# Attention weights kept for later chunks: turned by VectorE, written to DRAM and read back

## The chip, the cores and the metric

The kernel runs on one core of one Trainium2 chip. The metric is the device time of one execution in microseconds (us). Before the change three executions took 2239.99, 2240.82 and 2241.12 us, median 2240.82 us.

## The reference

Two layers in float32, one after the other. First an attention without softmax over four batches of 3008 rows, in which queries and keys are the same array `z` (64 wide); then a gated feed-forward layer over all 12032 rows:

```
scores = (z @ z.T) / 3008              # per batch, 3008 x 3008
attn   = maximum(scores, 0) ** 2
x      = u * (attn @ v)                # u, v: 3008 x 256
gate   = 1 / (1 + exp(-(x @ w_gate)))  # w_gate, w_val: 256 x 1536
out    = (gate * (x @ w_val)) @ w_out  # w_out: 1536 x 256
```

Since queries and keys are one array, `attn` is symmetric: the block of keys in chunk e against queries in chunk c is the transpose of the block of keys c against queries e.

## The kernel before

**Numbers.** TensorE multiplies in fp32r. To keep float32 accuracy every operand x is split into xh, its value in fp32r, and xl = x - xh, and each product is made of three matmuls (h*h, h*l, l*h). For the scores the two halves of `z` are stacked over the 128 partitions, so that two matmuls do it.

**Tiling.** Each batch has six chunks of 512 queries (the last has 448) and twelve pairs of 256 keys. One step is one (batch b, chunk c, pair k); there are 4 x 6 x 12 = 288 steps. All tiles of attention lie transposed: keys on partitions, queries along the free dimension. The gated layer runs one chunk behind: in step (b, c, k) it does feature block f = k of the chunk before, with 12 blocks of 128 features.

**A step on TensorE**, in this order: scores of the next step (`pe_scores`, L236, 4 matmuls, tile `sc`), attention times v of this step (`pe_pv`, L263, 12 matmuls into `acc`), the output product of an earlier feature block (`pe_out`, L330, 6 matmuls into `oacc`), and gate and value products (`pe_gv`, L297, 12 matmuls into `gv`): 34 matmuls, each with 512 columns (448 where the last chunk is concerned). `sc`, `acc`, `oacc` and `gv` have one PSUM buffer each.

**A step on the other engines**, in this order: ScalarE takes the sigmoid of `gv` and VectorE multiplies (`gate`, L312, tile `g`); for the next step ScalarE does relu and square of `sc` into `r`, VectorE casts `r` to `ah` and subtracts to `al` (`post_scores`, L247); ScalarE copies `g` to `hh` and VectorE subtracts to `hl` (`split_h`, L321). Once per chunk come the transposes of `u` (`prep_u`), the product with `u` (`make_x`), its split (`split_x`) and the transposes of the output (`finish`).

**Order.** The program is written out by hand: each engine takes its instructions in the order of the loop over `steps` (L427). All DMAs go through SP's queue, in that same order. During the first two chunks of batch 0 the weights of the gated layer, which arrive as float64 words, are loaded (`load_w`), narrowed to float32 (`narrow_w`: ScalarE one, VectorE five instructions, GpSimd one) and split (`split_w`: VectorE or ScalarE one, GpSimd one); `w_steps` (L371) says at which steps. In steps 14, 17 and 20 two pieces are narrowed.

**Memory.** The pool `const` holds the weights and, last, the tile `zero`, of 16 floats (64 bytes per partition); all other pools (z, v, `ah`, `al`, `hh`, `xh` and so on) lie behind it, and their tiles are multiples of 512 bytes.

Of the kernel before, what the change touches and what calls it, by code (L numbers as in the profile page):

```python
# [8 lines left out]
F32 = mybir.dt.float32  # L9
F32R = mybir.dt.float32r  # L10
# [3 lines left out]
AF = mybir.ActivationFunctionType  # L14
ALU = mybir.AluOpType
# [13 lines left out]
def kernel(  # L29
# [18 lines left out]
    DQ = z.shape[2]  # L50
# [128 lines left out]
    vraw_t, v_t = {}, {}  # L179
# [12 lines left out]
    def prep_v(b, k):  # L192
        t = vraw_t.pop((b, k))
        vh = vp.tile([P, 2, D], F32R, tag="vh", name="vh")
        vl = vp.tile([P, 2, D], F32R, tag="vl", name="vl")
        split(vh, vl, t, nc.gpsimd)
        v_t[b, k] = vh, vl

    def stack_v(b):
        vh, vl = v_t[b, NPAIR - 1]  # L200
        nc.scalar.activation(vh[64:128, 1, :], f32(vl[64:128, 1, :]), AF.Copy)


    uraw_t, u_t = {}, {}
# [25 lines left out]
    def early(b, c):  # L230
        return (b, c) == (0, 0)


    sc_t, a_t, acc_t, x_t = {}, {}, {}, {}

    def pe_scores(b, c, k):  # L236
        n = chunk(c)
        sc = ps.tile([P, 2, CH], F32, tag="gv" if early(b, c) and k % 2 else "sc", name="sc")
        kP = z_t[b, k // 2][0]
        qP, qQ = z_t[b, c]  # L240
        for j in range(2):
            o = (k % 2) * 256 + j * P
            nc.tensor.matmul(sc[:, j, 0:n], kP[:, o : o + P], qP[:, 0:n], start=True, stop=False)  # L243
            nc.tensor.matmul(sc[:, j, 0:n], kP[:, o : o + P], qQ[:, 0:n], start=False, stop=True)  # L244
        sc_t[b, c, k] = sc

    def post_scores(b, c, k):  # L247
        n = chunk(c)
        sc = sc_t.pop((b, c, k))
        r = one.tile([P, 2, CH], F32, tag="ut" if early(b, c) and k % 2 else "r", name="r")  # L250
        if early(b, c) and k % 3 == 2:
            ah = one.tile([P, 2, CH], F32R, tag="xh", name="ah")
            al = one.tile([P, 2, CH], F32R, tag="xl", name="al")
        else:
            ah = two.tile([P, 2, CH], F32R, tag="ah", name="ah")
            al = two.tile([P, 2, CH], F32R, tag="al", name="al")
        nc.scalar.activation(r[:, :, 0:n], sc[:, :, 0:n], AF.Relu, scale=scale)  # L257
        nc.scalar.activation(r[:, :, 0:n], r[:, :, 0:n], AF.Square)  # L258
        nc.vector.tensor_copy(ah[:, :, 0:n], r[:, :, 0:n])  # L259
        nc.vector.tensor_tensor(al[:, :, 0:n], r[:, :, 0:n], f32(ah[:, :, 0:n]), op=ALU.subtract)  # L260
        a_t[b, c, k] = ah, al

    def pe_pv(b, c, k):  # L263
        n = chunk(c)
# [56 lines left out]
    def split_h(b, c, f):  # L321
        n = chunk(c)
        g = g_t.pop((b, c, f))
        pool, tags = (vp, ("vh", "vl")) if (b, c) == (B - 1, NCH - 1) else (two, ("hh", "hl"))
        hh, hl = (pool.tile([P, CH], F32R, tag=tag, name=tag) for tag in tags)
        split(hh[:, 0:n], hl[:, 0:n], g[:, 0:n])
        h_t[b, c, f] = hh, hl

# [60 lines left out]
    with tc.manual_schedule():  # L389


        zero = const.tile([P, 16], F32, name="zero")
        nc.gpsimd.memset(zero, 0.0)
        nc.scalar.activation(zero, zero, AF.Sigmoid)
        idle = one.tile([P, CH], BF16, tag="ut", name="idle")
        nc.vector.memset(idle, 0.0)
        warm = ps.tile([P, 2, CH], F32, tag="acc", name="warm")

        def keep_warm(n):
            for _ in range(n):  # L400
# [24 lines left out]

        m1 = m2 = None
        for g, (b, c, k) in enumerate(steps):  # L427
            C = b * NCH + c
            ahead = g + (1 if C else 2)
            nxt = steps[ahead] if ahead < len(steps) and g != NPAIR - 1 else None  # L430
            if nxt:
                pe_scores(*nxt)
            if m1:
                gate(*m1)
            if k == 0 and C > 0:
                split_x(*chunks[C - 1])
            if nxt:
                post_scores(*nxt)
            if C == 0:
                if k + 2 < NPAIR:  # L440
                    prep_v(0, k + 2)
                if k + 4 < NPAIR:
                    load_v(0, k + 4)
                if k % 2 == 0 and k // 2 + 4 < NCH:
                    load_z(0, k // 2 + 4)
                if k % 2 == 0 and k // 2 + 2 < NCH:
                    prep_z(0, k // 2 + 2)
                if k % 2 == 1 and k // 2 + 3 < NCH:
# [12 lines left out]
            if m2:
                pe_out(*m2)
            m1, m2 = None, m1
            if C > 0:
                m1 = (*chunks[C - 1], k)
                pe_gv(*m1)

            weights(g)
            if c == NCH - 1 and b + 1 < B:
                if k == 0:  # L470
                    load_z(b + 1, 0)
                if k % 2 == 1:
# [76 lines left out]
```

## Time and profile before

| what | value |
|---|---|
| median of three runs | 2240.82 us |
| profiled execution, its own time | 2239.89 us |
| its span, first to last instruction | 2238.1 us |
| TensorE busy | 2204.5 us, 98%, 9762 matmuls |
| VectorE busy | 1169.5 us, 52% |
| ScalarE busy | 1002.3 us, 45% |
| GpSimd busy | 159.2 us, 7% |
| SP's DMA queue | 52.99 MB, 12.2% of the 16 DMA engines' span |
| mean granted TensorE clock | 0.993 |

Of a busy TensorE the distance from the start of one matmul to the start of the next counts, not the duration of one: matmuls overlap, and one that lasts 0.39 us is followed by the next after 0.23 us. A stretch is read by the starts of its first and last rows. PE is TensorE, DVE VectorE, ACT ScalarE, POOL GpSimd, SP the queue that issues all DMAs.

### The profile page before, as it was taken

The numbers are of one execution on the slowest core, as the hardware profiler recorded it, in microseconds if no ns is written. First come the engines' busy times: TensorE is split into PE (matmuls) and PEld (weight loads), VectorE is DVE, ScalarE is ACT, GpSimd is POOL, SyncE is SP. The second block draws the span as 40 slices with busy tenths as digits, with TensorE's granted clock in tenths as the row PEclk, the third lists the DMA queues.
The fourth block names the chain that finished last, engine by engine and source line by source line (L and its number), as shares of the span: only waits on it lengthen the run. The fifth ranks groups of instructions, "written<-read, shape, count | busy, mean of one in ns | idle before, by whom it ended". The sixth has DMA issues, their size and how long they took to land.

```text
span 2238.1 us, 23860 instructions
## 1 busy us (share of the span) xinstructions
PE 2204.5 (98%) x9762; PEld 1839.5 (82%) x9762; DVE 1169.5 (52%) x1451; ACT 1002.3 (45%) x1304; POOL 159.2 (7%) x107
## 2 busy tenths in 40 slices
PE   8889999999999999999999999999999999999998
PEld 5677888888888888888888888888888888888888
DVE  8996445456444444545644444445555444444543
ACT  6454444455444444435544444444554444444432
POOL 3441000013000000002200000000310000000000
PEclk9999999999999999999999999999999999999999
DMA  4221010021110100103101011010410110101101
GB/s 108 81 76 29 1 19 15 15 55 39 20 18 1 19 5 15 29 1 70 39 5 18 1 19 19 1 29 1 84 29 1 18 19 1 19 1 19 18 1 18
DMA packets 271054, 54.51 MB, mean 24 GB/s; under 512 B 250976, under 2 KB 269408, under 8 KB 270944
## 3 DMA queue, kind: packets, MB, share of 16 engines
q1 hardware_dynamic: 270944, 52.99, 12.2%
q8 instruction: 76, 1.25, 0.2%
q14 instruction: 34, 0.28, 0.0%
HBM read 40.63 MB, written 12.32 MB: 24 GB/s over the span
## 4 chain that ended last, share of the span: by engine, by line
PE 91%; DVE 7%; issue 1%; ACT 1%; DMA 0%; SPq 0%; DVEq 0%
PE gv L306 11%; PE gv L305 11%; PE gv L307 11%; PE acc L277 10%; PE acc L278 10%; PE acc L280 10%; PE oacc L347 6%; PE oacc L346 6%; PE oacc L348 5%; PE sc L243 5%; PE sc L244 5%; DVE al L260 1%; DVE ah L259 1%; DVE hl L82 1%; DVE wa L122 1%
## 5 line engine op out<-in xcount | busy, mean ns | idle before, releaser
L316 ACT ACTIVATE g<-gv 128x512 f32<-128x512 f32 (+1 forms) x288 | 169.4, 588 | 1003.1 <-PE gv L307 977.1
L317 DVE TENSOR_TENSOR g<-gv,g 128x512 f32<-128x512 f32 (+1 forms) x288 | 195.9, 680 | 586.9 <-ACT g L316 586.9
L305 PE MATMUL gv<-xh,wgv_h 128*128 128x512 f32 (+1 forms) x1152 | 449.0, 390 | 9.5 <-DVE g L317 9.4
L278 PE MATMUL acc<-al,vh 128*128 128x512 f32 (+1 forms) x1152 | 446.8, 388 | 6.2 <-DVE al L260 6.2
L306 PE MATMUL gv<-xl,wgv_h 128*128 128x512 f32 (+1 forms) x1152 | 449.3, 390 | 1.5 <-DVE xl L82 1.1
L277 PE MATMUL acc<-ah,vh 128*128 128x512 f32 (+1 forms) x1152 | 446.5, 388 | 3.3 <-DVE ah L259 2.0
L307 PE MATMUL gv<-xh,wgv_l 128*128 128x512 f32 (+1 forms) x1152 | 445.1, 386 | 0.0
L280 PE MATMUL acc<-ah,vl 128*128 128x512 f32 (+1 forms) x1104 | 428.3, 388 | 1.7 <-POOL vl L82 1.7
L259 DVE CAST ah<-r 128x1024 fp32r<-128x1024 f32 (+1 forms) x288 | 205.2, 712 | 420.8 <-ACT r L258 420.8
L260 DVE TENSOR_TENSOR al<-r,ah 128x1024 fp32r<-128x1024 f32 (+1 forms) x288 | 360.3, 1251 | 9.8
L257 ACT ACTIVATE r<-sc 128x1024 f32<-128x1024 f32 (+1 forms) x288 | 290.7, 1009 | 79.7 <-PE sc L244 78.5
L258 ACT ACTIVATE r<-r 128x1024 f32<-128x1024 f32 (+1 forms) x288 | 300.0, 1042 | 9.1
L305 PEld LDWEIGHTS gv<-xh,wgv_h 128*128 128x128 f32 x1152 | 217.6, 189 | 54.9 <-DVE g L317 10.6
L278 PEld LDWEIGHTS acc<-al,vh 128*128 128x128 f32 x1152 | 217.8, 189 | 48.7 <-DVE al L260 7.5
L277 PEld LDWEIGHTS acc<-ah,vh 128*128 128x128 f32 x1152 | 217.9, 189 | 46.0 <-ACT vh L81 2.5
L307 PEld LDWEIGHTS gv<-xh,wgv_l 128*128 128x128 f32 x1152 | 217.4, 189 | 43.7
L306 PEld LDWEIGHTS gv<-xl,wgv_h 128*128 128x128 f32 x1152 | 217.8, 189 | 42.4 <-DVE xl L82 3.4
L280 PEld LDWEIGHTS acc<-ah,vl 128*128 128x128 f32 x1104 | 208.8, 189 | 42.3 <-POOL vl L82 3.1
L243 PE MATMUL sc<-zP 128*128 128x512 f32 (+1 forms) x576 | 223.2, 387 | 4.5 <-DVE zP L174 4.4
L244 PE MATMUL sc<-zQ,zP 128*128 128x512 f32 (+1 forms) x576 | 222.6, 387 | 0.2 <-DVE zQ L175 0.2
L82 DVE TENSOR_TENSOR hl<-g,hh 128x512 fp32r<-128x512 f32 (+1 forms) x276 | 215.3, 780 | 0.7 <-ACT hh L81 0.7
L347 PE MATMUL oacc<-hl,wo_h 128*128 128x512 f32 (+1 forms) x552 | 215.1, 390 | 0.0
(54 smaller groups left out, 1670.3 us busy)
## 6 DMA issues: line engine op xcount, KB each, us to landing
vraw<-in_v_dram SPq DMA_DIRECT2D x44, 256.0 KB, 2.9
uraw<-in_u_dram SPq DMA_DIRECT2D x160, 64.0 KB, 2.4
out_dram<-osb SPq DMA_DIRECT2D x160, 64.0 KB, 2.0
zraw<-in_z_dram SPq DMA_DIRECT2D x80, 64.0 KB, 2.8
wraw<-in_moe_w_gate_dram SPq DMA_DIRECT2D x12, 256.0 KB, 2.7
wraw<-in_moe_w_val_dram SPq DMA_DIRECT2D x12, 256.0 KB, 3.1
wraw<-in_moe_w_out_dram SPq DMA_DIRECT2D x6, 512.0 KB, 3.6
uraw<-in_u_dram SPq DMA_DIRECT2D x32, 56.0 KB, 2.4
```

The lines of the kernel that those rows point to most:

```text
L243: nc.tensor.matmul(sc[:, j, 0:n], kP[:, o : o + P], qP[:, 0:n], start=True, stop=False)
L244: nc.tensor.matmul(sc[:, j, 0:n], kP[:, o : o + P], qQ[:, 0:n], start=False, stop=True)
L257: nc.scalar.activation(r[:, :, 0:n], sc[:, :, 0:n], AF.Relu, scale=scale)
L258: nc.scalar.activation(r[:, :, 0:n], r[:, :, 0:n], AF.Square)
L260: nc.vector.tensor_tensor(al[:, :, 0:n], r[:, :, 0:n], f32(ah[:, :, 0:n]), op=ALU.subtract)
L277: nc.tensor.matmul(o, vh[:, j, ds], ah[:, j, 0:n], start=(k == 0 and j == 0), stop=False)
L278: nc.tensor.matmul(o, vh[:, j, ds], al[:, j, 0:n], start=False, stop=last)
L280: nc.tensor.matmul(o, vl[:, j, ds], ah[:, j, 0:n], start=False, stop=False)
L305: nc.tensor.matmul(o, wh, xh[:, d, 0:n], start=(d == 0), stop=False)
L306: nc.tensor.matmul(o, wh, xl[:, d, 0:n], start=False, stop=False)
L307: nc.tensor.matmul(o, wl, xh[:, d, 0:n], start=False, stop=(d == NB - 1))
L347: nc.tensor.matmul(o, wh, hl[:, 0:n], start=False, stop=False)
```

## The change

The weights `r` of keys in a later chunk e than the queries' chunk c are kept for the time when e is the queries' chunk and c the keys' (`kept`, L80 of the new program; batch 0's chunk 0 keeps nothing). VectorE turns each 32x32 block of the tile (`turn`, two transposes of 128x512 per step), and DMAs of 32x16x32 put the blocks at their transposed places in a DRAM tile, in runs of 128 bytes, eight DMAs per step (six for the last pair, which has 192 keys). When chunk e comes, `load_back` reads each pair's tile in one DMA two steps ahead, and `pe_scores`, relu and square are left out for it (`back`, L84).

That concerns 110 of the 288 steps on either side: 30 of a batch's 72, and 20 in batch 0. The cast to `ah` moves from VectorE to ScalarE in steps that read back and in the whole of batch 0's chunk 1. `r` now has two buffers in all steps. The turned tiles use the buffers of `vraw`. The low part of v's last pair, whose second half is stacked into `vh`, is written in place by GpSimd, with no copy by ScalarE; the pool `vl` has a buffer less. `zero` grows from 64 to 512 bytes per partition, so that the pools behind it start at the same offset modulo 512 as the weights.

```diff
+    def kept(b, c, e):
+        return e > c and (b, c) != (0, 0)
+    def back(b, c, k):
+        return kept(b, k // 2, c)
...
     def pe_scores(b, c, k):
+        if back(b, c, k):
+            return
...
-        r = one.tile([P, 2, CH], F32, tag="ut" if early(b, c) and k % 2 else "r", name="r")
+        if back(b, c, k):
+            r = r_t.pop((b, c, k))
+        else:
+            r = two.tile([P, 2, CH], F32, tag="r", name="r")
+            nc.scalar.activation(r[:, :, 0:n], sc[:, :, 0:n], AF.Relu, scale=scale)
+            nc.scalar.activation(r[:, :, 0:n], r[:, :, 0:n], AF.Square)
...
-        nc.scalar.activation(r[:, :, 0:n], sc[:, :, 0:n], AF.Relu, scale=scale)
-        nc.scalar.activation(r[:, :, 0:n], r[:, :, 0:n], AF.Square)
-        nc.vector.tensor_copy(ah[:, :, 0:n], r[:, :, 0:n])
+        if back(b, c, k) or (b, c) == (0, 1):
+            nc.scalar.activation(ah[:, :, 0:n], r[:, :, 0:n], AF.Copy)
+        else:
+            nc.vector.tensor_copy(ah[:, :, 0:n], r[:, :, 0:n])
...
+    def turn(b, c, k):
+        r = r_t.pop((b, c, k))
+        e = k // 2
+        if not kept(b, c, e):
+            return
+        if (b, c, e) not in turned_t:
+            turned_t[b, c, e] = dram.tile([CH, CH], F32, name=f"turned_{b}_{c}_{e}")
+        rows = turned_t[b, c, e].rearrange("(T p) q -> p T q", p=32)
+        for j in range(2):
+            t = two.tile([P, CH], F32, tag="vraw", name="turned")
+            nc.vector.transpose(out=t, in_=r[:, j, :])
+            for g in range(4):
+                q = (k % 2) * 256 + j * P + 32 * g
+                if q < chunk(e):
+                    nc.sync.dma_start(
+                        rows[:, :, q : q + 32],
+                        t[32 * g : 32 * g + 32].rearrange("p (T q) -> p T q", q=32),
+                    )
+    def load_back(b, c, k):
+        n = chunk(c)
+        r = two.tile([P, 2, CH], F32, tag="r", name="r")
+        src = turned_t[b, k // 2, c][(k % 2) * 256 : (k % 2) * 256 + 256, 0:n]
+        nc.sync.dma_start(r[:, :, 0:n], src.rearrange("(j p) q -> p j q", p=P))
+        r_t[b, c, k] = r
...
-        zero = const.tile([P, 16], F32, name="zero")
+        zero = const.tile([P, 128], F32, name="zero")
...
             if nxt:
                 post_scores(*nxt)
+            if g + 2 < len(steps) and back(*steps[g + 2]):
+                load_back(*steps[g + 2])
...
             if m1:
                 split_h(*m1)
+            if nxt:
+                turn(*nxt)
             pe_pv(b, c, k)
```

TensorE, where batch 0's chunk 2 begins to read back; first before (L307 `pe_gv`, L243 and L244 `pe_scores`, L277 to L280 `pe_pv`):

```order
L307 MATMUL gv<-xh,wgv_l 128x512
L243 MATMUL sc<-zP 128x512
L244 MATMUL sc<-zQ,zP 128x512
L243 MATMUL sc<-zP 128x512
L244 MATMUL sc<-zQ,zP 128x512
L277 MATMUL acc<-ah,vh 128x512
```

Now, at the same place (L361 `pe_gv`, L331 to L334 `pe_pv`):

```order
L361 MATMUL gv<-xh,wgv_l 128x512
L331 MATMUL acc<-ah,vh 128x512
L332 MATMUL acc<-al,vh 128x512
L334 MATMUL acc<-ah,vl 128x512
L331 MATMUL acc<-ah,vh 128x512
```

The four matmuls of the scores are gone from between the two products; the rest keeps its order. Over the program TensorE has 440 matmuls fewer.

VectorE, one step of batch 0's chunk 1 in which one weight piece is narrowed, before (L317 `gate`, L259 and L260 `post_scores`, L82 `split_h`, L116 to L126 `narrow_w`):

```order
L317 TENSOR_TENSOR g<-gv,g 128x512
L259 CAST ah<-r 128x1024
L260 TENSOR_TENSOR al<-r,ah 128x1024
L82 TENSOR_TENSOR hl<-g,hh 128x512
L116 TENSOR_SCALAR wa<-wa 128x512
L119 TENSOR_SCALAR wa<-wa 128x512
L122 SCALAR_TENSOR_TENSOR wa<-wraw,wa 128x512
L125 TENSOR_SCALAR wb<-wa 128x512
L126 SCALAR_TENSOR_TENSOR wb<-wraw,wb 128x512
```

The same step now (L371 `gate`, L284 `post_scores`, L95 `split_h`, L301 `turn`, L129 to L139 `narrow_w`):

```order
L371 TENSOR_TENSOR g<-gv,g 128x512
L284 TENSOR_TENSOR al<-r,ah 128x1024
L95 TENSOR_TENSOR hl<-g,hh 128x512
L301 STREAM_TRANSPOSE turned<-r 128x512 x2
L129 TENSOR_SCALAR wa<-wa 128x512
L132 TENSOR_SCALAR wa<-wa 128x512
L135 SCALAR_TENSOR_TENSOR wa<-wraw,wa 128x512
L138 TENSOR_SCALAR wb<-wa 128x512
L139 SCALAR_TENSOR_TENSOR wb<-wraw,wb 128x512
```

The cast has gone to ScalarE, and two transposes stand between `hl` and the weights.

SP's queue at the end of batch 0's chunk 1, before (L92 and L99 `load_w`, L212 `load_u`, L359 `finish`):

```order
L92 DMA wraw<-in_moe_w_gate_dram 128x2x256
L92 DMA wraw<-in_moe_w_val_dram 128x2x256
L212 DMA uraw<-in_u_dram 32x16x32 x8
L99 DMA wraw<-in_moe_w_out_dram 128x2x512
L359 DMA out_dram<-osb 32x16x32 x8
```

The same stretch now (L105 and L112 `load_w`, L305 `turn`, L228 `load_u`, L314 `load_back`, L415 `finish`):

```order
L105 DMA wraw<-in_moe_w_gate_dram 128x2x256
L105 DMA wraw<-in_moe_w_val_dram 128x2x256
L305 DMA turned_1_5_1326<-turned 32x16x32 x8
L228 DMA uraw<-in_u_dram 32x16x32 x8
L112 DMA wraw<-in_moe_w_out_dram 128x2x512
L305 DMA turned_1_5_1326<-turned 32x16x32 x6
L314 DMA r<-turned_1_2_841 128x2x512 x2
L415 DMA out_dram<-osb 32x16x32 x8
```

Eight stores of a turned tile now stand ahead of the loads of u and of the last piece of `w_out`, and two read-backs ahead of the output's stores.

## Rows read from the trace of the kernel before

**Rows 1.** The page's chain that ended last, share of the span by engine.

```profile
PE 91%; DVE 7%; issue 1%; ACT 1%; DMA 0%; SPq 0%; DVEq 0%
```

**Rows 2.** TensorE's waits, first 300 us: us in total, times, longest; the largest.

```profile
PE gv L305 <- DVE g L317: 9.4, 3, 3.3
```

**Rows 3.** TensorE's waits, 300 us to the end: the largest.

```profile
PE gv L306 <- DVE xl L82: 0.7, 1, 0.7
```

**Rows 4.** Timeline, TensorE, one step of 512 columns: start us, us, instruction.

```profile
300.50 0.39 PE L243 MATMUL sc<-zP 128*128 128x512 f32 x1
...
301.41 0.39 PE L277 MATMUL acc<-ah,vh 128*128 128x512 f32 x1
...
304.13 0.39 PE L346 MATMUL oacc<-hh,wo_h 128*128 128x512 f32 x1
...
305.50 0.39 PE L305 MATMUL gv<-xh,wgv_h 128*128 128x512 f32 x1
...
308.25 0.39 PE L243 MATMUL sc<-zP 128*128 128x512 f32 x1
```

**Rows 5.** Timeline, TensorE, a step whose queries are the last chunk.

```profile
1014.68 0.36 PE L243 MATMUL sc<-zP 128*128 128x448 f32 x1
...
1015.49 0.37 PE L277 MATMUL acc<-ah,vh 128*128 128x448 f32 x1
...
1017.97 0.39 PE L346 MATMUL oacc<-hh,wo_h 128*128 128x512 f32 x1
```

**Rows 6.** Timeline, TensorE, gate and value products of a last chunk, and what follows.

```profile
577.93 0.36 PE L305 MATMUL gv<-xh,wgv_h 128*128 128x448 f32 x1
...
580.34 0.39 PE L243 MATMUL sc<-zP 128*128 128x512 f32 x1
```

**Rows 7.** Timeline, VectorE, one steady step; in brackets the idle time before, its releaser.

```profile
305.63 0.68 DVE L82 TENSOR_TENSOR hl<-g,hh 128x512 fp32r<-128x512 f32 x1
309.08 0.69 DVE L317 TENSOR_TENSOR g<-gv,g 128x512 f32<-128x512 f32 x1 [2.76 <-ACT g L316]
```

**Rows 8.** Groups by shape: busy us, mean ns of one, idle before.

```profile
L223 DVE STREAM_TRANSPOSE ut<-uraw 128x512 f32<-128x512 f32 x40 | 25.9, 687 | 0.0
...
L81 ACT ACTIVATE xh<-ut 128x1024 fp32r<-128x1024 f32 x20 | 21.1, 1053 | 8.2 <-DVE ut L285 8.2
```

**Rows 9.** Timeline, SP's queue, the eight stores of one chunk's output.

```profile
198.97 4.16 SPq L359 DMA_DIRECT2D out_dram<-osb  x8
```

**Rows 10.** The page's DMA issues: count, KB each, median us from issue to landing.

```profile
out_dram<-osb SPq DMA_DIRECT2D x160, 64.0 KB, 2.0
...
wraw<-in_moe_w_out_dram SPq DMA_DIRECT2D x6, 512.0 KB, 3.6
```

**Rows 11.** Windows: length, busy of PE, PEld, DVE, ACT, POOL; clock; DMA share, GB/s.

```profile
196.00:204.00 8.00, 8.00 (x37) 6.60 (x36) 4.69 (x7) 3.46 (x5) 0.00 (x0) 1.00 0.40 63
212.00:220.00 8.00, 8.00 (x37) 6.59 (x36) 3.47 (x5) 3.21 (x4) 0.00 (x0) 1.00 0.00 0
```

**Rows 12.** Timeline, VectorE, one step of batch 0's chunk 1 with weights.

```profile
114.86 1.48 DVE L259 CAST ah<-r 128x1024 fp32r<-128x1024 f32 x1
116.37 1.23 DVE L260 TENSOR_TENSOR al<-r,ah 128x1024 fp32r<-128x1024 f32 x1
117.51 1.80 DVE L82 TENSOR_TENSOR hl<-g,hh 128x512 fp32r<-128x512 f32 x1
...
122.02 0.68 DVE L317 TENSOR_TENSOR g<-gv,g 128x512 f32<-128x512 f32 x1
```

**Rows 13.** Timeline, GpSimd, the same step.

```profile
114.49 1.30 POOL L129 TENSOR_TENSOR wa<-wa,wb 128x512 f32<-128x512 f32 x1 [3.40 <-DVE wb L126]
116.53 2.24 POOL L141 TENSOR_TENSOR wo_l<-wa,wo_h 128x512 fp32r<-128x512 f32 x1 [0.74 <-ACT wo_h L140]
```

**Rows 14.** Timeline, SP's queue, the last loads of batch 0's chunk 1.

```profile
161.88 4.05 SPq L212 DMA_DIRECT2D uraw<-in_u_dram  x8
...
170.56 0.38 SPq L99 DMA_DIRECT2D wraw<-in_moe_w_out_dram  x1
```

More of the change, by code (lines that the diff above doesn't have):

```diff
@@ L68 @@
     vp = ctx.enter_context(tc.tile_pool(name="vp", bufs=NPAIR))
+    vlp = ctx.enter_context(tc.tile_pool(name="vlp", bufs=NPAIR - 1))
     ps = ctx.enter_context(tc.tile_pool(name="ps", bufs=1, space=PSUM))
+    dram = ctx.enter_context(tc.tile_pool(name="dram", bufs=1, space=bass.MemoryType.DRAM))
     def f32(ap):
         return ap.bitcast(F32)
+    def kept(b, c, e):
+        return e > c and (b, c) != (0, 0)
+    def back(b, c, k):
+        return kept(b, k // 2, c)
     wgv_h = const.tile([P, NF, 2, NB, P], F32R, name="wgv_h")
@@ L194, in prep_v @@
         vh = vp.tile([P, 2, D], F32R, tag="vh", name="vh")
-        vl = vp.tile([P, 2, D], F32R, tag="vl", name="vl")
-        split(vh, vl, t, nc.gpsimd)
+        if k < NPAIR - 1:
+            vl = vlp.tile([P, 2, D], F32R, tag="vl", name="vl")
+            split(vh, vl, t, nc.gpsimd)
+        else:
+            vl = one.tile([P, 1, D], F32R, tag="vlast", name="vlast")
+            nc.scalar.activation(vh, t, AF.Copy)
+            nc.gpsimd.tensor_tensor(vl[:, 0, :], t[:, 0, :], f32(vh[:, 0, :]), op=ALU.subtract)
+            stacked = vh[64:128, 1, :]
+            nc.gpsimd.tensor_tensor(stacked, t[64:128, 1, :], f32(stacked), op=ALU.subtract)
         v_t[b, k] = vh, vl
-    def stack_v(b):
-        vh, vl = v_t[b, NPAIR - 1]
-        nc.scalar.activation(vh[64:128, 1, :], f32(vl[64:128, 1, :]), AF.Copy)
     uraw_t, u_t = {}, {}
@@ L231, in early @@
         return (b, c) == (0, 0)
-    sc_t, a_t, acc_t, x_t = {}, {}, {}, {}
+    sc_t, r_t, a_t, acc_t, x_t = {}, {}, {}, {}, {}
     def pe_scores(b, c, k):
+        if back(b, c, k):
+            return
         n = chunk(c)
@@ L248, in post_scores @@
         n = chunk(c)
-        sc = sc_t.pop((b, c, k))
-        r = one.tile([P, 2, CH], F32, tag="ut" if early(b, c) and k % 2 else "r", name="r")
+        sc = sc_t.pop((b, c, k), None)
+        if back(b, c, k):
[4 more added lines that the diff above has]
+            nc.scalar.activation(r[:, :, 0:n], r[:, :, 0:n], AF.Square)
         if early(b, c) and k % 3 == 2:
@@ L256, in post_scores @@
             al = two.tile([P, 2, CH], F32R, tag="al", name="al")
-        nc.scalar.activation(r[:, :, 0:n], sc[:, :, 0:n], AF.Relu, scale=scale)
-        nc.scalar.activation(r[:, :, 0:n], r[:, :, 0:n], AF.Square)
-        nc.vector.tensor_copy(ah[:, :, 0:n], r[:, :, 0:n])
+        if back(b, c, k) or (b, c) == (0, 1):
+            nc.scalar.activation(ah[:, :, 0:n], r[:, :, 0:n], AF.Copy)
+        else:
+            nc.vector.tensor_copy(ah[:, :, 0:n], r[:, :, 0:n])
         nc.vector.tensor_tensor(al[:, :, 0:n], r[:, :, 0:n], f32(ah[:, :, 0:n]), op=ALU.subtract)
         a_t[b, c, k] = ah, al
+        r_t[b, c, k] = r
+    turned_t = {}
+    def turn(b, c, k):
[21 more added lines that the diff above has]
+        nc.sync.dma_start(r[:, :, 0:n], src.rearrange("(j p) q -> p j q", p=P))
+        r_t[b, c, k] = r
     def pe_pv(b, c, k):
@@ L323, in split_h @@
         g = g_t.pop((b, c, f))
-        pool, tags = (vp, ("vh", "vl")) if (b, c) == (B - 1, NCH - 1) else (two, ("hh", "hl"))
-        hh, hl = (pool.tile([P, CH], F32R, tag=tag, name=tag) for tag in tags)
+        last = (b, c) == (B - 1, NCH - 1)
+        hh = (vp if last else two).tile([P, CH], F32R, tag="vh" if last else "hh", name="hh")
+        low = last and f < NF - 1
+        hl = (vlp if low else two).tile([P, CH], F32R, tag="vl" if low else "hl", name="hl")
         split(hh[:, 0:n], hl[:, 0:n], g[:, 0:n])
@@ L449 @@
                     turn_z(0, k // 2 + 3)
-                if k == NPAIR - 2:
-                    stack_v(0)
             if m1:
                 split_h(*m1)
+            if nxt:
+                turn(*nxt)
             pe_pv(b, c, k)
@@ L481 @@
                 prep_v(b, NPAIR - 1)
-            if c == 0 and b > 0 and k == 1:
-                stack_v(b)
         last = chunks[-1]
```

## The prediction, made before the changed kernel ran

> **What bounds the kernel now.** I read the chain that ended last first: 91% of the span is TensorE's [rows 1]. TensorE's waits, taken in two stretches, say where it ever stands still: after 300 us its largest wait in total is 0.7 us, while in the first 300 us one kind alone, gate and value products that wait for VectorE's `g`, costs 9.4 us [rows 2, 3]. So there are two regimes. From about 190 us on, the time is the number of matmuls times their distance: one step of 512 columns goes from 300.50 to 308.25, 7.75 us for 34 matmuls, 0.228 us each [rows 4]. VectorE there has 2.76 us of idle time in one piece per step [rows 7]. Before that, in batch 0's chunk 1, VectorE narrows weights and has no gap: from cast to the next `g` its rows follow one another [rows 12].
>
> The window with the eight stores of an output and the one without any DMA both hold 37 matmuls in 8.00 us [rows 11]: transfers cost TensorE nothing there.
>
> **The change part by part.** The sum is made against the profiled execution, 2239.9 us (span 2238.1 and 1.8 around it), 0.9 below the median shown.
>
> *Scores removed.* 110 steps lose 4 matmuls each. Where queries have 512 columns, the four take 301.41 - 300.50 = 0.91 us [rows 4]; in the last chunk 1015.49 - 1014.68 = 0.81 us [rows 5]. Chunk c reads back 2c steps, in batch 0 two fewer from chunk 1 on: 38 steps are of the last chunk (8 + 3 x 10), 72 of the others (12 + 3 x 20). 72 x 0.91 + 38 x 0.81 = 96.3 us. The steady stretch has no other wait to hide behind, so all of it comes off: -96.3.
>
> *What has to stay hidden in steady steps.* VectorE gets two transposes in 110 steps, 2 x 0.687 = 1.37 us [rows 8], directly before its idle 2.76 us [rows 7]. Left are 1.39 us; where the step also transposes u or the output (two more), 2.75 of 2.76 are taken, and `g` behind them still has some 3 us, since its product's next matmul comes at 305.50 + 7.75, and `g` ends at 309.77. Without that cover the price would be 1.37 us x 110 = 151 us. ScalarE loses relu and square in read-back steps and gains one copy of 1.05 us [rows 8]. SP gets eight issues, 4.16 us as for the eight stores of an output, which have the same shape [rows 9], in a step of 7.75; with eight loads of u or eight stores of the output behind them it has some 8.3, and it catches up in the next step, which has 3.6 to spare. The stores land in 2.0 us [rows 10]; the turned tile's two buffers are wanted again one step later, so that from the first transpose 7.75 us are there for 0.69 + 2.1 + 2.0. The read-back has the form of the 512 KB load of `w_out`, 3.6 us [rows 10]. It is issued two steps ahead, behind the wait for the buffer of `r` that `al` or the transposes release; what stands behind it in SP's queue (turned stores, u, output) is not due sooner than half a step later. Its source was stored eight steps before at the nearest. In the read-back step `ah` needs no TensorE, so `al` is early by the 2 us of relu and square. Cost taken: 0; bounds 0 to 5.
>
> On small stores the trace has this: eight of 64 KB in runs of 128 bytes fill 0.40 of the 16 DMA engines over 8 us, 3.2 us of all of them [rows 11], so eight more per step fit in 7.75 us twice. [...]
>
> *Batch 0's chunk 1.* The cast leaves VectorE, but is worth less than its 1.48 us: it starts at 114.86, while GpSimd's addition runs until 115.79 [rows 12, 13], and the next subtraction would wait for GpSimd as well (`hl` takes 1.80 us beside GpSimd's split, 0.68 in a steady step [rows 7, 12]). So 1.48 - 0.93 = 0.55, taken as 0.6, is saved per step, in 11 steps with weights: -6.6. Eight of them gain transposes, 8 x 1.37 = +11.0. In the last such step but one the loads of u and of `w_out` stand behind eight stores: before, u's were issued at 161.88, a step ahead, and `w_out`'s at 170.56 [rows 14]; now SP needs 4.2 for the stores and 4.05 for u, so that the piece lands 0.69 + 4.2 + 4.05 + 3.6 = 12.5 us after the first transpose begins. VectorE wants it a step later: 7.16 from cast to next `g` and 0.6 for `g` [rows 12], 0.8 longer by the change, and behind the next step's transposes and those of u, 2.75: 11.3. That is +1.2, taken as +1.0. Net +5.4. Bounds: -5.3 (11 whole casts of 1.48 gone against 11.0 of transposes) to +12.0 (transposes and late load, nothing saved).
>
> *The 512-byte offset.* `zero` grows, so weights of the gated layer and what is multiplied with them, 64 bytes apart modulo 512 before, agree. In 512-column steps the products whose operands agree already run 12 matmuls in 304.13 - 301.41 = 2.72 us; gate and value take 308.25 - 305.50 = 2.75, the output product's six 1.37 against 1.36 [rows 4]. Brought to the same distance: 0.04 x 240 steps = -9.6. With 448 columns the agreeing ones are the slower: 2.48 for 12 against 2.41 [rows 5, 6], so up to 0.07 and half of it for the output, 0.105 x 48 steps = +5.0. I take both, -4.6; the bounds are the ends, -9.6 and +5.0.
>
> [...]
>
> *The rest.* The copies that stacked v's last pair (one per batch on ScalarE) and the shorter subtraction on GpSimd stand in steps with idle time: 0.
>
> Sum: 2239.9 - 96.3 + 5.4 - 4.6 = **2144.4 us**.
>
> **Rivals.** (A) The offset does nothing. For it: distances differ by about 1% only, and with the opposite sign at 448 columns, so they may belong to the products and not to their addresses. Against: both agreeing products are the quicker at 512 [rows 4]. Time 2149.0. (B) The weights' stretch gets worse: ScalarE's `ah`, behind relu and square, comes when VectorE is free and nothing is saved there, +12.0 in place of +5.4, and the offset gives nothing: 2239.9 - 96.3 + 12.0 = 2155.6. For it: VectorE has no gap there [rows 12]. Against: the cast shows no wait for ScalarE before it [rows 12], so `r` is there early. (C) The other side: the path transpose, eight stores, buffer free becomes the bound of the 110 turned steps. Stores into 2 KB rows of a scratch tile appear nowhere in the trace; the output's go into 1 KB rows. The gain is used up when each turned step is 96.3 / 110 = 0.88 us longer, thus when eight stores take 8.63 us, 2.7 times the 3.2 of [rows 11]. At three times, 9.6 us: 110 x 1.85 = +203, 2347 us. Against: the same run length lands in 2.0 us [rows 10]. (D) The scores are not really saved, because something else sets the step: excluded by 2.76 us of idle on VectorE and by ScalarE's lighter step.
>
> **Numbers.** Forecast 0.55, A 0.32, B 0.09, C 0.04. The low end takes the offset's best and some relief of VectorE: 2239.9 - 96.3 - 9.6 - 3 = 2131. The high end is B with some 2 us for the hidden terms' bound, 2158. This leaves C and the tails out. A measurement of this kernel can tell 0.2% (4.5 us) from no change; all but C are faster by far: faster 0.95, within 0.2% 0.01, slower 0.04.
>
> **What would show it.** TensorE with 440 matmuls fewer and no wait beyond 1 us in total after 200 us per cause; a read-back step of 30 matmuls at 6.84 us. VectorE's idle before `g` in a turned step near 1.4 us. `g`'s wait on TensorE in the first 200 us grown by some 5 us. Twelve gate and value matmuls in 2.72 us, or, for A, still 2.75. The prediction is wrong if turned steps last over 7.75 us, if read-backs release ScalarE's `ah` late, or if SP's queue shows waits for transposes that TensorE's chain ends in.

## The result, and the profile after

The changed kernel takes 2143.05 us (median of four executions, 2141.06 to 2144.6), the kernel before beside it 2240.4 us (2239.92 to 2241.12). The ratio is 0.9565, 95% interval 0.9548 to 0.9581. The profiled execution took 2141.06 us with a span of 2139.2 us; it is the quickest of the four, so that differences read from its stretches and differences of medians can disagree by some 2 us. The forecast was 2144.4 us.

First the page of the changed kernel: busy time and instructions of each engine, the chain that ended last, and the DMA issues that are new.

```profile
PE 2103.4 (98%) x9322; PEld 1755.0 (82%) x9322; DVE 1210.9 (57%) x1549; ACT 895.9 (42%) x1202; POOL 154.9 (7%) x111
...
PE 91%; DVE 4%; ACT 2%; DMA 1%; issue 1%; SPq 1%; POOL 0%; DVEq 0%; ACTq 0%
...
turned<-turned SPq DMA_DIRECT2D x842, 64.0 KB, 1.9
r<-turned SPq DMA_DIRECT2D x72, 512.0 KB, 4.1
```

TensorE has 440 matmuls fewer (9762 before) and still carries 91% of the chain [rows 1]. SP's queue moves three times the bytes, 163.41 MB for 52.99, and stands at 35.8% of the DMA engines for 12.2%. A read-back lands 4.1 us after its issue, where 3.6 were foretold.

To see where the time went, both executions are cut where batch 0's chunks 0 and 1 end (at the start of the split of `x`, `xl`, for the next chunk). Each row below is one stretch: its limits, its length, busy us of PE, PEld, DVE, ACT and POOL with their instructions, granted clock, DMA share, GB/s. Before:

```profile
0.00:79.89 79.89, 64.22 (x226) 45.94 (x227) 70.77 (x79) 42.17 (x53) 33.71 (x25) 0.89 0.43 104
79.89:186.59 106.70, 95.57 (x390) 76.71 (x389) 101.78 (x121) 55.95 (x77) 46.99 (x28) 0.94 0.22 66
186.59:2238.10 2051.51, 2044.73 (x9149) 1716.89 (x9147) 996.97 (x1252) 904.19 (x1176) 78.46 (x54) 1.00 0.11 19
```

After:

```profile
0.00:77.43 77.43, 64.03 (x228) 45.15 (x228) 69.01 (x78) 42.92 (x53) 35.10 (x26) 0.91 0.45 108
77.43:189.03 111.60, 96.04 (x387) 75.97 (x388) 98.62 (x126) 66.83 (x88) 40.80 (x28) 0.94 0.45 104
189.03:2139.20 1950.17, 1943.33 (x8709) 1633.89 (x8707) 1043.31 (x1346) 786.17 (x1063) 78.98 (x57) 1.00 0.35 74
```

Chunk 0 is 2.5 us shorter, chunk 1 4.9 longer, the rest 101.3 shorter, together -98.9. In the rest TensorE is idle for 6.8 us in either kernel (2051.51 - 2044.73, 1950.17 - 1943.33): so its gain is matmuls gone or closer together, although the DMA engines went from 0.11 to 0.35 of their time and VectorE has 46 us more work.

TensorE's waits after, first 300 us, then from 300 us on (total, times, longest):

```profile
PE gv L359 <- DVE g L371: 14.7, 6, 4.6
```

```profile
PE gv L360 <- DVE xl L95: 1.3, 4, 0.7
```

These answer to [rows 2, 3]: 9.4 became 14.7. In the steady stretch 0.7 became 1.3, a little over the 1 us per cause that the forecast had set as a sign, and still nothing worth a term; waits for `g` come to 0.5 us there.

One step of 512 columns on TensorE, to be laid beside [rows 4]:

```profile
320.00 0.39 PE L261 MATMUL sc<-zP 128*128 128x512 f32 x1
...
323.63 0.39 PE L402 MATMUL oacc<-hh,wo_h 128*128 128x512 f32 x1
...
324.99 0.39 PE L359 MATMUL gv<-xh,wgv_h 128*128 128x512 f32 x1
...
327.71 0.39 PE L261 MATMUL sc<-zP 128*128 128x512 f32 x1
```

The step takes 7.71 us for 7.75; gate and value 2.72 for 2.75, the output product 1.36 for 1.37, the rest as before.

VectorE in the steady stretch, to be laid beside [rows 7]: two read-back steps, an ordinary step, a turned step, and one that turns and also transposes `u`. In brackets the idle time before an instruction.

```profile
306.32 0.69 DVE L371 TENSOR_TENSOR g<-gv,g 128x512 f32<-128x512 f32 x1 [4.02 <-ACT g L370]
...
313.12 0.69 DVE L371 TENSOR_TENSOR g<-gv,g 128x512 f32<-128x512 f32 x1 [4.02 <-ACT g L370]
...
328.54 0.69 DVE L371 TENSOR_TENSOR g<-gv,g 128x512 f32<-128x512 f32 x1 [2.72 <-ACT g L370]
...
336.24 0.69 DVE L371 TENSOR_TENSOR g<-gv,g 128x512 f32<-128x512 f32 x1 [1.51 <-ACT g L370]
...
341.14 1.30 DVE L301 STREAM_TRANSPOSE turned<-r 128x512 f32<-128x512 f32 x2
...
343.95 0.69 DVE L371 TENSOR_TENSOR g<-gv,g 128x512 f32<-128x512 f32 x1 [0.32 <-ACT g L370]
```

A read-back step lasts 313.12 - 306.32 = 6.80 us (30 matmuls; 6.84 foretold). The idle piece before `g`, 2.72 in an ordinary step, shrinks to 1.51 in a turned one and to 0.32 where `u` is transposed as well. A piece is left in each of these steps, and TensorE's waits for `g` of 0.5 us in the whole steady stretch say that it is used up hardly anywhere.

Batch 0's chunk 1 is where time was lost. VectorE, one step with weights, beside [rows 12]:

```profile
110.14 0.68 DVE L371 TENSOR_TENSOR g<-gv,g 128x512 f32<-128x512 f32 x1
110.74 1.99 DVE L284 TENSOR_TENSOR al<-r,ah 128x1024 fp32r<-128x1024 f32 x1
...
114.35 1.29 DVE L301 STREAM_TRANSPOSE turned<-r 128x512 f32<-128x512 f32 x2
...
118.58 0.68 DVE L371 TENSOR_TENSOR g<-gv,g 128x512 f32<-128x512 f32 x1
```

From `g` to `g` it is 8.44 us, with no gap over 0.15. The cast of 1.48 is gone, but the subtraction `al` grew from 1.23 to 1.99: it now starts 0.37 after GpSimd's addition, which runs from 110.37 to 111.65. In five other steps of chunk 1 `al` waits for ScalarE's `ah` instead, 5.3 us in all and 1.9 at most; before, VectorE made `ah` itself.

```profile
110.37 1.28 POOL L142 TENSOR_TENSOR wa<-wa,wb 128x512 f32<-128x512 f32 x1 [2.88 <-DVE wb L139]
```

SP's queue at the end of chunk 1, beside [rows 14]: the loads of `u` and `w_out` stand behind eight stores.

```profile
165.75 4.17 SPq L305 DMA_DIRECT2D turned<-turned  x8
170.02 4.17 SPq L228 DMA_DIRECT2D uraw<-in_u_dram  x8
174.30 0.42 SPq L112 DMA_DIRECT2D wraw<-in_moe_w_out_dram  x1
```

The piece of `w_out` is issued at 174.30; VectorE then waits 2.06 us, until 179.04, for ScalarE's first instruction on it. Such waits for weights come to 3.5 us in chunk 1, and one for `u` to 0.4.

### The profile page after: what moved, and what is told of

Its sections match the earlier page's. It is cut to its first block, busy times and chain, and to the rows that moved or that the text cites. A ratio compares the mean times of both kernels' runs of the same rounds, so it can differ in the third digit from the quotient of the medians.

```text
span 2139.2 us, 24723 instructions
## 1 busy us (share of the span) xinstructions
PE 2103.4 (98%) x9322; PEld 1755.0 (82%) x9322; DVE 1210.9 (57%) x1549; ACT 895.9 (42%) x1202; POOL 154.9 (7%) x111
## 3 DMA queue, kind: packets, MB, share of 16 engines
q1 hardware_dynamic: 745440, 163.41, 35.8%
## 4 chain that ended last, share of the span: by engine, by line
PE 91%; DVE 4%; ACT 2%; DMA 1%; issue 1%; SPq 1%; POOL 0%; DVEq 0%; ACTq 0%
PE gv L360 12%; PE gv L359 12%; PE gv L361 12%; PE acc L331 11%; PE acc L332 11%; PE acc L334 10%; PE oacc L403 6%; PE oacc L402 6%; PE oacc L404 6%; PE sc L262 3%; PE sc L261 3%; DVE al L284 1%; DMA wraw<-in_moe_w_val_dram 1%; ACT r L273 0%; ACT r L272 0%
## 5 line engine op out<-in xcount | busy, mean ns | idle before, releaser
L371 DVE TENSOR_TENSOR g<-gv,g 128x512 f32<-128x512 f32 (+1 forms) x288 | 195.7, 679 | 567.1 <-ACT g L370 566.9
L359 PE MATMUL gv<-xh,wgv_h 128*128 128x512 f32 (+1 forms) x1152 | 447.5, 388 | 16.2 <-DVE g L371 15.2
L331 PE MATMUL acc<-ah,vh 128*128 128x512 f32 (+1 forms) x1152 | 446.3, 387 | 1.7 <-DVE ah L283 1.7
L361 PE MATMUL gv<-xh,wgv_l 128*128 128x512 f32 (+1 forms) x1152 | 446.1, 387 | 0.0
L334 PE MATMUL acc<-ah,vl 128*128 128x512 f32 (+1 forms) x1056 | 409.1, 387 | 1.6 <-POOL vl L95 1.6
L284 DVE TENSOR_TENSOR al<-r,ah 128x1024 fp32r<-128x1024 f32 (+1 forms) x288 | 363.7, 1263 | 35.1 <-ACT ah L281 25.3
L359 PEld LDWEIGHTS gv<-xh,wgv_h 128*128 128x128 f32 x1152 | 217.4, 189 | 61.8 <-DVE g L371 19.6
L283 DVE CAST ah<-r 128x1024 fp32r<-128x1024 f32 (+1 forms) x166 | 115.7, 697 | 254.2 <-ACT r L273 254.2
L331 PEld LDWEIGHTS acc<-ah,vh 128*128 128x128 f32 x1152 | 217.5, 189 | 44.7 <-ACT vh L213 1.6
L361 PEld LDWEIGHTS gv<-xh,wgv_l 128*128 128x128 f32 x1152 | 217.5, 189 | 41.1
L334 PEld LDWEIGHTS acc<-ah,vl 128*128 128x128 f32 x1056 | 199.6, 189 | 40.1 <-POOL vl L95 2.7
L403 PE MATMUL oacc<-hl,wo_h 128*128 128x512 f32 (+1 forms) x576 | 222.2, 386 | 0.0
L402 PE MATMUL oacc<-hh,wo_h 128*128 128x512 f32 (+1 forms) x576 | 222.0, 385 | 0.0
L404 PE MATMUL oacc<-hh,wo_l 128*128 128x512 f32 (+1 forms) x576 | 221.9, 385 | 0.0
L95 DVE TENSOR_TENSOR hl<-g,hh 128x512 fp32r<-128x512 f32 (+1 forms) x288 | 215.2, 747 | 9.2 <-ACT hh L94 9.2
L272 ACT ACTIVATE r<-sc 128x1024 f32<-128x1024 f32 (+1 forms) x178 | 181.8, 1021 | 55.7 <-PE sc L262 53.9
L273 ACT ACTIVATE r<-r 128x1024 f32<-128x1024 f32 (+1 forms) x178 | 187.6, 1054 | 5.7
```

Of the source, the lines that this page charges most:

```text
L331: nc.tensor.matmul(o, vh[:, j, ds], ah[:, j, 0:n], start=(k == 0 and j == 0), stop=False)
L334: nc.tensor.matmul(o, vl[:, j, ds], ah[:, j, 0:n], start=False, stop=False)
L359: nc.tensor.matmul(o, wh, xh[:, d, 0:n], start=(d == 0), stop=False)
L361: nc.tensor.matmul(o, wl, xh[:, d, 0:n], start=False, stop=(d == NB - 1))
L371: nc.vector.tensor_tensor(g[:, 0:n], gv[:, 1, 0:n], g[:, 0:n], op=ALU.mult)
L402: nc.tensor.matmul(o, wh, hh[:, 0:n], start=(f == 0), stop=False)
```

## Experiments

My theory was the forecast's sum: scores off TensorE, turning paid for in chunk 1 alone, a small gain from the offset. Each run had the kernel before beside it on the same chip (median 2239.87 us in both groups: e1 to e4, e5 to e8). Differences "to the changed kernel" are to its median of 2143.05 us, lengths of stretches are of the profiled executions, cut as above. Where nothing in the steady stretch was changed, its length repeats within 1.6 us: 1950.17 in the changed kernel, 1948.95 in e3 and 1950.52 in e7.

### e1_offset_back: the changed kernel with `zero` small again

```diff
-        zero = const.tile([P, 128], F32, name="zero")
+        zero = const.tile([P, 16], F32, name="zero")
```

> The changed kernel with the tile zero at 64 bytes again, so that the gated layer's weights and their moving operands differ by 64 bytes modulo 512. Theory (the offset counts): twelve gate and value matmuls of 512 columns go back from 2.72 to 2.75 us and the six of the output from 1.36 to 1.37, those of 448 columns become quicker; 4.6 us more than 2143.1 us, 2147.7. Rival A (the distances belong to the products, not to the offset): 2143.1 us, distances as in the changed kernel.

Measured: 2147.4 us (2146.7 to 2149.74), ratio to before 0.9588 [0.9575, 0.9601], 4.35 more than the changed kernel. TensorE's gate and value products, with 512 and with 448 columns, up to what follows them:

```profile
305.91 0.39 PE L359 MATMUL gv<-xh,wgv_h 128*128 128x512 f32 x1
...
308.66 0.39 PE L331 MATMUL acc<-ah,vh 128*128 128x512 f32 x1
...
580.26 0.36 PE L359 MATMUL gv<-xh,wgv_h 128*128 128x448 f32 x1
...
582.66 0.39 PE L261 MATMUL sc<-zP 128*128 128x512 f32 x1
```

The twelve are back at 2.75 us with 512 columns, and at 2.40 with 448, where the changed kernel has 2.43:

```profile
576.49 0.37 PE L359 MATMUL gv<-xh,wgv_h 128*128 128x448 f32 x1
...
578.92 0.39 PE L261 MATMUL sc<-zP 128*128 128x512 f32 x1
```

The window of the rest, cut at the same place:

```profile
191.54:2147.90 1956.36, 1948.76 (x8709) 1634.19 (x8707) 1042.18 (x1346) 785.82 (x1063) 79.31 (x57) 1.00 0.38 74
```

It has the same 8709 matmuls as the changed kernel and takes 6.2 us longer. Rival A (the offset does nothing) fell.

### e2_offset_alone: the kernel before with the large `zero`

```diff
-        zero = const.tile([P, 16], F32, name="zero")
+        zero = const.tile([P, 128], F32, name="zero")
```

> The kernel before with zero at 512 bytes and nothing else. Theory: 4.6 us less than 2240.4 us, 2235.8, with twelve gate and value matmuls of 512 columns in 2.72 us. Rival A: 2240.4 us, still 2.75.

Measured: 2233.85 us (2233.17 to 2234.59), ratio 0.9972 [0.996, 0.9983], -6.0 us. Its twelve gate and value products of 512 columns take 2.72 us, from the first to what follows, and the window of the rest is cut as before:

```profile
306.05 0.39 PE L305 MATMUL gv<-xh,wgv_h 128*128 128x512 f32 x1
...
308.77 0.39 PE L243 MATMUL sc<-zP 128*128 128x512 f32 x1
```

```profile
187.77:2232.80 2045.03, 2038.00 (x9149) 1717.01 (x9147) 996.68 (x1252) 903.46 (x1176) 78.28 (x54) 1.00 0.10 19
```

The rest is 6.5 us shorter than before with the same 9149 matmuls. Both ways round the offset is worth some 6 us in the steady stretch. The runs know only two cases, 64 bytes apart and in agreement; whether 512 is the measure, or 128 or 256 would do as well, they do not show. e1 and e2 also give the scores by themselves: 2051.51 - 1956.36 = 95.2 us at the old offset, 2045.03 - 1950.17 = 94.9 at the new one.

### e3_loads_first: in chunk 1 the stores are issued behind the loads of weights

```diff
-                    nc.sync.dma_start(
-                        rows[:, :, q : q + 32],
-                        t[32 * g : 32 * g + 32].rearrange("p (T q) -> p T q", q=32),
+                    stores.append(
+                        (
+                            rows[:, :, q : q + 32],
+                            t[32 * g : 32 * g + 32].rearrange("p (T q) -> p T q", q=32),
+                        )
                     )
+        if (b, c) != (0, 1):
+            store()
...
             weights(g)
+            store()
```

`store` issues what the list holds and empties it; `weights` issues the loads of weights.

> The changed kernel; in batch 0's chunk 1 the stores of a turned tile are issued behind the loads of weights and of u of the same step, not ahead of them. Theory (the late loads make up most of what chunk 1 costs): VectorE's waits for weight pieces and for u in that chunk, 0.23 + 1.18 + 2.06 + 0.38 = 3.9 us, go, and with them up to 3.9 us of the time: 2139 to 2141 us. Rival (VectorE has no slack there anyway and only its own instructions count): those waits go, but others take their place, 2143 us.

Measured: 2143.98 us (2142.74 to 2145.31), ratio 0.9571 [0.9558, 0.9584]: no gain. VectorE's waits in chunk 1 (88 to 185 us) of this kernel:

```profile
DVE al L284 <- ACT ah L281: 6.5, 5, 2.2
DVE turned L301 <- DMA turned<-turned: 5.2, 6, 1.4
```

The waits for weights are gone; stores that are issued later release the turned tiles later, and VectorE waits for these instead, while `al` waits 6.5 us for `ah` where the changed kernel has 2.8 in the same window. So this order exchanges one wait for others and gets nothing back. What the late loads would cost without that exchange it does not show.

### e4_turn_after_gate: in chunk 1 a tile is turned a step later, behind `g`

```diff
+        pending = []
...
+            while pending:
+                turn(*pending.pop())
             if nxt:
                 post_scores(*nxt)
...
-            if nxt:
+            if nxt and C == 1:
+                pending.append(nxt)
+            elif nxt:
```

> The changed kernel; in batch 0's chunk 1 VectorE turns a tile one step later, behind the gate's product g and ahead of the subtraction al, while GpSimd adds the narrowed weights; the stores move with it, behind the loads of the step before. Theory (al waits some 0.7 us for GpSimd in each such step, and loads come late): 8 x 0.7 = 5.6 us of blocked time are filled with transposes and the late loads go; between 2136 and 2140 us. Rival (the transposes are themselves held up by GpSimd, or al waits for ScalarE's ah instead): 2143 us or more.

Measured: 2134.76 us (2131.83 to 2136.49), ratio 0.9528 [0.9515, 0.9541], 8.3 less than the changed kernel, better than expected. VectorE of this kernel, then GpSimd in the same step:

```profile
112.29 0.69 DVE L371 TENSOR_TENSOR g<-gv,g 128x512 f32<-128x512 f32 x1
112.89 1.29 DVE L301 STREAM_TRANSPOSE turned<-r 128x512 f32<-128x512 f32 x2
114.11 1.18 DVE L284 TENSOR_TENSOR al<-r,ah 128x1024 fp32r<-128x1024 f32 x1
...
119.69 0.68 DVE L371 TENSOR_TENSOR g<-gv,g 128x512 f32<-128x512 f32 x1
```

```profile
112.52 1.29 POOL L142 TENSOR_TENSOR wa<-wa,wb 128x512 f32<-128x512 f32 x1 [2.80 <-DVE wb L139]
```

The step takes 7.40 us for 8.44. The transposes last 1.29 beside GpSimd's addition, as long as behind it in the changed kernel (1.29 at 114.35), while the subtraction that now follows them is down from 1.99 to 1.18. So this order puts beside GpSimd's addition what it did not slow. That an instruction reads a single tile is not enough for that: the cast to `ah`, which reads one as the transposes do, took 1.48 beside the addition before [rows 12, 13] and takes 0.69 in the steady stretch, as at 303.76 of the same trace. Why the addition spared the transposes and not the cast the runs do not show.

TensorE's waits for `g` from 88 to 200 us fell from 14.7 to 7.9 us. The edit does two things, and both can be seen: over chunk 1 the twelve subtractions take 16.3 us for 19.1, 2.8 less, and VectorE's waits for late weights and `u` fall from 3.9 to 0.8 us, without the waits for turned tiles of e3. Which part of the 8.3 us belongs to which was not separated.

### e5_no_turn: no transposes and no stores; read-backs take other rows

```diff
-        src = turned_t[b, k // 2, c][(k % 2) * 256 : (k % 2) * 256 + 256, 0:n]
+        k0 = 256 * min(k, 9)
+        src = u[b, k0 : k0 + 512, :].rearrange("(i h) d -> i (h d)", h=2)[:, 0:n]
...
-                turn(*nxt)
+                r_t.pop(nxt)
```

> The changed kernel without transposes and without stores; what is read back are rows of u in the same 512 KB shape, so the attention weights of 110 steps are wrong data. Theory (transposes and stores are hidden in all steady steps): from the start of chunk 2 of batch 0 to the end the time is that of the changed kernel within 2 us; only chunk 1 gets shorter, by 6 to 8 us: 2135 to 2138 us. Rival (each turned step costs TensorE something, 0.1 us or more): 11 us or more less, below 2132.

Measured: 2130.03 us (2129.24 to 2130.83), ratio 0.9509 [0.9493, 0.9525], 13.0 less than the changed kernel. The rest of its profile:

```profile
177.49:2128.20 1950.71, 1943.81 (x8709) 1633.68 (x8707) 920.94 (x1142) 785.88 (x1063) 78.61 (x57) 1.00 0.20 48
```

VectorE has 122 us less to do there (1043.31 - 920.94) and the stretch is as long as in the changed kernel, 1950.71 for 1950.17. So in the steady stretch transposes and stores are hidden, to within the 1.6 us by which it repeats; the read-backs are still there, and no run takes them away. What is gained in the profiles, 11.0 us, is in chunk 1: 177.49 - 77.07 = 100.4 us for 111.6, more than the 6 to 8 us I had expected.

### e6_chunk1_keeps_nothing: tiles of batch 0's chunk 1 are not kept

```diff
-        return e > c and (b, c) != (0, 0)
+        return e > c and (b, c) not in ((0, 0), (0, 1))
```

> The changed kernel, where batch 0's chunk 1 keeps nothing either: eight steps turn nothing and eight later steps compute their scores again, 6 x 0.91 + 2 x 0.81 = 7.1 us of TensorE more. Theory (turning in chunk 1 costs 5 to 6 us there): the two nearly balance, 2144 us. If the turning there costs nothing: 2150 us. If it costs 10 us or more: 2140 us or less.

Measured: 2134.74 us (2134.41 to 2135.37), ratio 0.953 [0.9516, 0.9544], 8.3 less than the changed kernel where I had expected about the same. Chunk 0 ends at 77.53, chunk 1 where this window of the rest begins:

```profile
177.15:2132.70 1955.55, 1949.19 (x8741) 1640.02 (x8739) 1046.18 (x1354) 794.67 (x1071) 79.29 (x57) 1.00 0.35 72
```

Chunk 1 lasts 99.6 us (177.15 - 77.53) for 111.6, so turning costs 12.0 us there (11.2 by e5); eight more steps compute scores later, which costs 5.4 (1955.55 - 1950.17) where I had worked out 7.1. Keeping these eight tiles was a loss of 6.6 us in the profiles, as placed. With e4's place for the turn it is about even, 2134.76 us.

### e7_cast_on_dve: in chunk 1 the cast to `ah` stays on VectorE

```diff
-        if back(b, c, k) or (b, c) == (0, 1):
+        if back(b, c, k):
```

> The changed kernel, with batch 0's chunk 1 casting r to ah on VectorE as before. Theory of the prediction (0.6 us saved per step by ScalarE's copy): 12 x 0.6 = 7 us more, 2150 us. If the whole cast with its blocked time of 1.4 us was saved: 17 us more, 2160. Rival (the copy on ScalarE saves nothing, al waits for ah instead): 2143 us.

Measured: 2150.8 us (2150.71 to 2151.61), ratio 0.9602 [0.9588, 0.9617], 7.7 more than the changed kernel, as expected. In its profile chunk 0 ends at 79.60 and chunk 1 at 198.38. Chunk 1 is 7.2 us longer (118.8), chunk 0 2.2 us: its last step but one already casts the first tile of chunk 1. That cast takes 0.69 us and the subtraction behind it 2.17 for 1.22, together 1.6; the other 0.6 stands ahead of it. The rest, 2148.9 - 198.38 = 1950.5, is as in the changed kernel. So the move is worth having, although `al` now waits for ScalarE's `ah` here and there.

### e8_stores_twice: each store is issued a second time, to another DRAM tile

```diff
-                    nc.sync.dma_start(
-                        rows[:, :, q : q + 32],
+                    for to in (rows, again):
+                        nc.sync.dma_start(
+                            to[:, :, q : q + 32],
...
```

> The changed kernel with every store of a turned tile issued twice, the second into another DRAM tile. SP then issues sixteen stores in a turned step, 16 x 0.52 = 8.3 us in a step of 7.75. Theory (the path of the stores is near its bound, and SP's issue time sets it): turned steps become 8.3 us or a little more, 110 x 0.6 = 66 us more, about 2209 us, and VectorE waits for the buffers of the turned tiles. Rival (the stores have ample room, since buffers and steps without turning absorb it): 2143 to 2155 us. Rival (small stores are slow in the DMA engines themselves): far more, above 2260 us.

Measured: 2359.15 us (2354.42 to 2361.91), ratio 1.053 [1.0514, 1.0545], 216 more than the changed kernel, far more than expected. VectorE in two turned steps, SP's queue between, and the waits of the whole span:

```profile
603.28 0.71 DVE L303 STREAM_TRANSPOSE turned<-r 128x512 f32<-128x512 f32 x1 [3.68 <-DMA again<-turned]
...
612.02 0.71 DVE L303 STREAM_TRANSPOSE turned<-r 128x512 f32<-128x512 f32 x1 [3.66 <-DMA again<-turned]
```

```profile
604.34 0.51 SPq L308 DMA_DIRECT2D again<-turned  x1
604.89 0.49 SPq L308 DMA_DIRECT2D turned<-turned  x1
...
609.77 0.51 SPq L308 DMA_DIRECT2D again<-turned  x1
```

```profile
DVE turned L303 <- DMA again<-turned: 382.2, 120, 6.1
...
PE gv L362 <- DVE g L374: 138.8, 48, 8.3
```

Rival C's mechanism, brought about on purpose: SP's queue has no gap, one store per 8.74 / 16 = 0.546 us, and sixteen take the whole step of 8.74. The last store of the tile turned at 603.28 is issued at 609.77, and the transpose that waits for its buffer starts at 612.02, 2.25 us later; in the changed kernel a store lands 1.9 us after its issue. VectorE waits for a buffer, `g` comes behind the transpose, and TensorE waits for `g`. Windows of this step and the next (granted clock, DMA share and GB/s are the last three figures):

```profile
603.28:612.02 8.74, 7.46 (x23) 6.39 (x24) 4.29 (x6) 2.35 (x4) 0.00 (x0) 0.61 0.70 120
612.02:620.74 8.72, 8.72 (x42) 7.56 (x41) 4.29 (x7) 4.07 (x5) 0.00 (x0) 1.00 0.70 120
```

The DMA engines are busy for 0.70 of the step, not full. In the first of the two, a wait of TensorE for `g` ends that had begun before it and lasted 5.63 us:

```profile
604.56 0.74 PE L362 MATMUL gv<-xh,wgv_h 128*128 128x448 f32 x1 [5.63 <-DVE g L374]
...
609.21 0.63 PE L261 MATMUL sc<-zP 128*128 128x512 f32 x1
```

The granted clock of that window is 0.61, and from 605.85 us on the gate and value products of 448 columns follow each other at 0.37 us, so that the twelve take 609.21 - 604.56 = 4.65 us where the changed kernel has 2.43, 0.20 each. In the second window, which has no such wait, the clock is 1.00. So this wait was paid a second time, by 2.2 us in slower matmuls; over the whole execution the granted clock is 0.965 for 0.993. My expectation had left that out, and the read-backs that stand behind the stores. The time lies in the range that I had given to slow small stores; the rows speak for the queue, which takes 0.546 us per store here and took 4.17 / 8 = 0.52 in the changed kernel, while that buffer came free within 2.25 us of its last store's issue. How the 216 us divide over clock, read-backs and stores I did not separate.

## Why the prediction was right

| term | predicted, us | measured, us |
|---|---|---|
| scores of 110 steps | -96.3 | -95.2 and -94.9 (before to e1, e2 to after; the rest) |
| offset | -4.6 | -6.2 and -6.5 (e1 and e2, the rest); by medians -4.35 and -6.0 |
| turning in chunk 1, with late loads | +12.0 | +12.0 (e6, chunk 1), +11.2 (e5) |
| cast off VectorE in chunk 1 | -6.6 | -7.2 (e7, chunk 1) |
| steady transposes, stores, read-backs | 0 (0 to 5) | 0 for transposes and stores (e5); read-backs not taken apart |
| chunk 0 | not counted | -2.5 (e7: -2.2) |
| sum | -95.5 | -98.9 (profiled executions), -97.35 (medians) |

**Scores.** Right in mechanism and in size. The distances of four matmuls, read in one step before [rows 4, 5] and taken 110 times, gave 1.3 us too much; what the read-backs cost, if anything, lies in that difference.

**What has to stay hidden.** Right: the idle piece before `g` [rows 7] took the transposes, with 1.51 us left for the 1.39 worked out, and 0.32 where almost nothing was foretold. That the cover makes the work free is shown by e5: where there is cover, taking the work away gains nothing (1950.71 us for 1950.17), and in chunk 1, which has none, it gains 11.2 us. The waits that the forecast listed as signs of trouble are small: VectorE's turned tiles wait 5.6 us for their buffer in the whole span, ScalarE's `ah` 2.7 us for a read-back.

**Chunk 1.** The net, +4.9 for +5.4, is right. That a cast of 1.48 us was worth only some 0.6 a step because the subtraction behind it then lasts longer beside GpSimd's addition shows in the rows: `al` took 1.99 for 1.23, and the step is 8.44 us for 7.76 (7.16 from cast to `g` and 0.6 for `g`), +0.68 where 1.37 - 0.6 = 0.77 was reckoned. TensorE's wait for `g` grew by 5.3 us, foretold as some 5. The late loads came, as VectorE's waits of 3.9 us, but e3 did not give them a price: it put other waits in their place. So the +12.0 of the forecast, 11.0 for transposes and 1.0 for late loads, is confirmed as a sum and not by its parts, and that it is met to a tenth is luck.

**Offset.** Right in sign at both widths, and mis-sized at 448 columns. I had given those products the 2.48 us of the agreeing products there [rows 5, 6]; they went to 2.43, from 2.40 in e1. The 2.48 was a slow step: in the next one of the same trace the agreeing products take 2.43 as well.

```profile
1022.92 0.36 PE L277 MATMUL acc<-ah,vh 128*128 128x448 f32 x1
...
1025.35 0.39 PE L346 MATMUL oacc<-hh,wo_h 128*128 128x512 f32 x1
```

Thus +5.0 should have been 48 x 0.045 = +2.2, and -9.6 + 2.2 = -7.4 is nearer to the -6.2 and -6.5 measured. By rival A the term would be 0; e1 and e2 differ from that by 4.35 and 6.0 us with the same matmuls. Why 512 and 448 columns answer with opposite sign was not tried.

**Not counted.** The first tile of chunk 1 is cast in chunk 0's last step but one, and that cast moved as well; the forecast had counted 11 steps inside chunk 1 only. Chunk 0 gives -2.5 of the -3.4 by which the sum of the profiled executions fell short, and e7 puts 1.6 of that down to this cast.

**Rivals.** A fell with e1 and e2. B's condition (nothing saved by the cast) fell with e7, though its mechanism is there: `al` waits for `ah` for 5.3 us in chunk 1. D fell with the scores' 95 us. C did not happen, but e8 shows how near it was: doubling eight stores per step is enough, since SP issues one per 0.546 us and a step has 7.7. The forecast took its margin, 2.7 times, from the DMA engines' share [rows 11]; the queue that issues them has only 7.7 / 4.17 = 1.8, because eight stores take 4.17 us of it. The small runs themselves did no harm that shows: the stores of 128-byte runs land in 1.9 us, like the output's.

Both e4 and e6 beat the two kernels (2134.76 and 2134.74 us). They get back the same loss, so their gains do not add; keeping fewer of chunk 1's tiles with e4's order was not tried.

## What to carry to other kernels

When TensorE bounds a stretch, work that was moved to an idle piece of another engine cost nothing here as long as a piece was left in every step (1950.17 us with transposes and stores, 1950.71 without, e5): measure the piece in the fullest step, not in the mean. Price the stretch where that engine has no idle piece by itself, because the same edit was free in 102 steps and cost 1.5 us in each of eight (12.0 us, e6). And take the margin of a store path from the queue that issues it as well as from the DMA engines: in e8 the queue was full, at one store per 0.546 us, while the engines were 0.70 busy.

## What the runs showed of the hardware

- The distance of matmuls changed by about 1% with how weights and moving operand lie to each other: twelve of 512 columns take 2.75 us where they differ by 64 bytes modulo 512 and 2.72 where they agree, twelve of 448 columns 2.40 and 2.43 (e1 and the changed kernel). Worth 4.35 us (e1) and 6.0 us (e2) in all. Other offsets were not tried.
- SP issued one 64 KB store of 128-byte runs per 0.546 us while the DMA engines were 0.70 busy (e8): there the queue was full, and the engines were not.
- After a wait of 5.63 us on TensorE the granted clock was 0.61 in the window of that step, and twelve matmuls of 448 columns took 4.65 us for 2.43 (e8), so that the stall cost more than its own length.
- Beside GpSimd's addition VectorE's subtraction of two tiles took 1.99 us and 1.18 behind it (e4), the cast of one tile 1.48 [rows 12] and 0.69 in the steady stretch, two transposes 1.29 either way (e4).
